# A planned order searched anew around the w_out loads, and the last output tile evicted in three parts

## The chip, the core and the metric

The kernel runs on one core of a Trainium2 chip. The core has a matrix engine (TensorE, PE in the profile, with its weight loads listed apart as PEld), a vector engine (DVE), a scalar engine (ACT), GpSimd (POOL) and SyncE (SP), which here only issues DMAs. Each engine works through its own list of instructions in order, and waits on semaphores where it needs another engine or a transfer. The metric is the device time of one execution in microseconds (us).

## The reference

A retention layer (attention without softmax, with a decay per head) feeds a two-layer feed-forward network. 8 batches, 8 heads, 576 positions, head size 64; 4608 tokens of width 512; the hidden width is 2048.

```python
scores = scale * np.matmul(q, k.transpose(0, 1, 3, 2))
gamma = 1.0 - 2.0 ** (-5.0 - np.arange(H))
rel = pos[:, None] - pos[None, :]
Dmat = np.where(rel >= 0, gamma[:, None, None] ** rel[None], 0.0)
x = np.matmul(scores * Dmat, v)        # then [B, H, S, D] -> [B*S, H*D]
h = x @ w_in                           # 512 -> 2048
g = np.where(h > 0, h, np.exp(np.minimum(h, 0)) - 1)
out = g @ w_out                        # 2048 -> 512, float32
```

## The kernel before

**Attention.** The sequence is cut into stretches of 256 positions (and a rest of 64 for each batch, gathered four batches at a time). Decay is put into q and k as powers of gamma, so that a stretch needs only masked scores, values and a running state. The first two batches are cut once more, into eight "units" u0 to u7 of 256 positions by four heads: u0 and u1 are the two halves of the first stretch, u2 and u3 of the second, u4 to u7 the same for the second batch. A unit n is made by these steps: loads `ldq`, `ldk`, `ldv` (256 KB each, issued by SP into raw tiles `r`); scaled casts `cq0`, `cq1` of q (line 559), plain casts `kk0`, `kk1` of k (568) and scaled casts `vs0`, `vs1` of v (582); a transposition, which for u0 to u4 is done on PE (`Tn_0`, `Tn_1`, line 605, copied out of PSUM as `cp`, line 611) and for u5 to u7 by a transposing DMA (`tr5` to `tr7`, line 594, issued by SP); then scores `sc`, state `st` and output `iv` on PE, a mask on DVE (965), sums of the state and their casts `us` and `ub` (916, 886, 904), and copies of the result into x, `xc` (1001). From u4 on, these PE steps are merged: A4 begins u4, A5 ends u4 and begins u5, iv5 ends u5, A6 begins u6, A7 ends u6 and begins u7.

**Feed-forward.** Tokens are worked on in 16 blocks: 14 of 256 tokens (4 of them made of units), the last two of 512. `F1_b_p` (function `ffn1`) multiplies block b by a slice of w_in into one PSUM bank; ACT takes the exponential, ACT or DVE the other branch, DVE joins them into g. `F2_b_t_c_n` (function `ffn2`) multiplies 128 tokens (tile t) of g by w_out rows from 128c on, 4 chunks of 128 rows at a time, and adds up over 16 such chunks. The sum is copied out of PSUM by ACT or DVE (`oc`, line 1179) and stored by SP (`so`, line 1187). The last tile of the last block is done in two halves of 256 columns. `rows_of` gives the pieces in which a tile is stored: one of 128 rows, or two of 64 for the gathered rests.

**Weights.** w_in comes in five DMAs (`wi0` to `wi4`) and w_out in four (`wo0` to `wo3`, 512 KB each in bf16), all issued by POOL, which makes their descriptors in software. F1 with p = 0 needs `wi0`, p = 1 `wi1`, p = 2 and 3 `wi2`, p = 4 and 5 `wi3`, the rest `wi4`. F2 with c = 0, 4, 8, 12 needs `wo0`, `wo1`, `wo2`, `wo3`.

**What sets the order.** `Plan.run` (line 73 on) is a list scheduler in the program itself. At build time it gives every step a start by assumed costs, and the emitted program is the list of steps of each engine in that order. `AT` gives steps an earliest start in the plan, `RANKS` moves their priority. Both shape only the order of each engine's list: on the chip an engine takes the next instruction as soon as its semaphores allow. Where the plan sees PE idle in the first 50 us, it puts in matmuls on zeros ("fillers", lines 1273 to 1277), with which PE stays busy.

**Holds.** `HOLD = {"ldq4": "wo0", "ldq6": "wo1"}` delays two loads on the chip: POOL copies one column of the named part of `w_out_sb` into the raw tile (line 403), so this copy waits until that part has landed, and the load into the same tile waits for the copy. SP issues in order, so all later loads wait behind a held one. POOL's list in this stretch is: ... `wi4`, `vs0_3`, `wo0`, `wo1`, `wo2`, hold of ldq4, tables for the later stretches (iotas and a mask, lines 515 to 526), hold of ldq6, `wo3`, then the casts of u4.

PE's list up to the end of the units begins: 7 matmuls on zeros ("warm"), T0, T1, sc0, st0, sc1, iv0, st1, iv1, T2, st2, T3_0, sc2, T3_1, F1_0_0, F1_0_1, iv2, sc3, st3, F1_0_2, F1_0_3, iv3, F1_0_4, F1_0_5, then F1 of block 1 and the rest of block 0, F2 of blocks 0 and 1 with T4, A4, A5, iv5 between them, F1_2_0, A6, F1_2_1 and so on.

Of the kernel before, what the change touches and what calls it, by code (L numbers as in the profile page):

```python
# [17 lines left out]
P = 128  # L18
# [17 lines left out]
class Plan:  # L36
# [6 lines left out]
    def add(self, *a, **kw):  # L43
        op = Op(*a, **kw)
        self.ops.append(op)
        for key in op.use:
            self.users.setdefault(key, []).append(op)
            op.turn += self.owner.get(key, [])
        for cls, key, *_ in op.take:
            self.owner[key] = [op]  # L50
            if cls not in FREE:
                op.turn += self.takers.get(cls, [])
                self.takers[cls] = [op]
        return op
# [152 lines left out]
JOINT = True  # L207
BD_ACT = 0.6
FILL = 0.6
TWO, STEP = 2, 4  # L210
KK = {"ACT": 0.37}
VV = {"POOL": 0.62, "DVE": 0.5}
# [15 lines left out]
UAPART = (5, 7)  # L228
HOLD = {"ldq4": "wo0", "ldq6": "wo1"}
VLATE = (0, 1)  # L230
AT = {"wi0": 7.1, "wi1": 8.0, "wi2": 8.5, "wi3": 11.0, "wi4": 15.0, "wo0": 16.4, "wo1": 16.1, "wo2": 19.3, "wo3": 31.3, "so_0_1_0_0": 74, "so_1_0_0_0": 74, "so_1_1_0_0": 74, "so_2_0_0_0": 76, "so_2_1_0_0": 81.47, "F2_3_1_0_0": 78.57, "g_2_6": 63.17, "md_3_3": 66.87, "md_1_7": 35.82, "us5_0": 44.11, "ex_2_4": 55.85, "ex_2_2": 53.77, "xc1_u4": 43.93, "xc0_4": 82.16, "g_1_3": 27.7, "xc1_u3": 22.43, "F2_3_0_8_0": 78.02, "md_0_7": 36.11, "F1_6_6": 119.86, "tr0_5": 66.58, "md_2_2": 56.94, "ex_6_5": 119.61, "md_0_1": 21.97, "mask1_7": 117.16, "md_0_5": 25.96, "F2_4_0_8_0": 93.26, "cv7": 47.1, "F1_0_5": 22.04, "cq11": 5.73, "ub5_1": 47.68, "F1_0_3": 19.14, "g_1_7": 36.97, "vs1_7": 47.23, "cq00": 4.92, "cq16": 39.58, "ex_0_3": 22.04, "kk1_4": 33.96, "tr6": 42.78, "md_1_0": 25.42}
RANKS = {"us1_0": -2, "F1_0_1": 4, "mask0_7": 2, "g_2_1": -2, "md_3_3": 8, "A7": -4, "cv1_5": -4, "cv1_6": 4, "mask1_u6": 8, "so_5_0_0_0": -8, "md_0_2": -8, "ex_2_7": 2, "xc0_u7": -8, "F1_2_6": -8, "A4": 2, "F2_3_0_4_0": -8, "ub0_0": -4, "kk1_2": 4, "g_0_5": 4, "F2_1_1_0_0": 8}
FREE = ("f", "e", "em", "g", "ot")
SURE = 3
ATT = ((0, 0), (0, 1), (1, 0), (1, 1), (2, 0), (2, 1), (3, 0), (3, 1), (4, 0), (4, 1), "X",
# [12 lines left out]
def kernel(  # L248
# [12 lines left out]
    B, H, S, D = q.shape  # L261
    DM, DF = moe_w_in.shape
    HP = H // 2
    C = 64
    NC = 4
    R = C // 2
    TB = NC * C
# [11 lines left out]
    def mm(*a, **kw):  # L279
        return pin(nc.tensor.matmul(*a, **kw))  # L280
# [54 lines left out]
    add = plan.add  # L335
# [4 lines left out]
    def T(cls, key, shape, dt):  # L340
        return (cls, key, shape, dt)
# [8 lines left out]
    for n, key in enumerate(ATT):  # L350
        it = Work()
# [18 lines left out]
    blocks, place = [], 0  # L370
    for i, keys in enumerate(FFN):
        blk = Work()
# [775 lines left out]
    def rows_of(blk, t):  # L1148
        it, half = blk.its[t // 2], t % 2
        if not it.tail:  # L1150
            return [(0, P, it.b * S + it.T * TB + half * P)]
        return [(j * C, C, (it.b + 2 * half + j) * S + 2 * TB) for j in range(2)]

    tilesof2, byp = [], {}

    def ffn2(blk, t, f0, f1, rank, n0=0, n1=DM):
        pkey, okey = ("p", blk.i, t, n0), ("ot", blk.i, t, n0)
        per, width = 512 // blk.w, n1 - n0
        gs = range(f0 // per, (f1 - 1) // per + 1)

        def emit(op):
            pm = tiles[pkey][:, :width]
            for ft in range(f0, f1):
                g = tiles["g", blk.i, ft // per]
                o = (ft % per) * blk.w + t * P
                mm(pm, g[:, o : o + P], w_out_sb[:, ft, n0:n1], start=(ft == 0), stop=(ft == NFT - 1))

        op = add(f"F2_{blk.i}_{t}_{f0}_{n0}", {"PE": 0.216 * (f1 - f0) * width / DM},
                 [blk.g[p] for p in gs] + [w_out_ld[ft] for ft in range(f0, f1)], emit, rank,
                 take=[] if f0 else [T("f", pkey, [P, DM], FP32)],  # L1170
                 use=([pkey] if f0 else []) + [("g", blk.i, p) for p in gs], after=chain.get(2))
        chain[2] = op
        if f0 == 0:
            tilesof2.append([])
            byp[pkey] = tilesof2[-1]
        byp[pkey].append(op)
        if f1 == NFT:
            def emit_o(op):
                pin(copy[op.eng](tiles[okey][:, :width], tiles[pkey][:, :width]))  # L1179

            oc = add(f"oc_{blk.i}_{t}_{n0}", {"ACT": 0.59 if width == DM else 0.36,
                                              "DVE": (0.66 if width == DM else 0.36, 0.3)}, [op], emit_o, rank,
                     take=[T("ot", okey, [P, DM], FP32)], use=[pkey], banks=[(pkey, 0)])
            for lo, n, i0 in rows_of(blk, t):
                def emit_s(op, lo=lo, n=n, i0=i0):
                    eng = nc.scalar if op.eng == "ACT" else nc.sync
                    pin(eng.dma_start(out[i0 : i0 + n, n0:n1], tiles[okey][lo : lo + n, :width]))

                add(f"so_{blk.i}_{t}_{n0}_{lo}", {OUT: 0.5}, [oc], emit_s, -2, use=[okey],
                    dma=(0.67 * n / P * width / DM, 8))  # L1190
# [38 lines left out]
    for blk in blocks:  # L1229
        base, n = (blk.at + len(blk.its)) * 16 + 1, blk.w // P  # L1230
        if blk.i < TWO:
            for o in blocks[:TWO] if blk.i == TWO - 1 else ():
                o.base = (o.at + len(o.its)) * 16 + 1
            for c in range(0, NFT, STEP) if blk.i == TWO - 1 else ():
                for o in blocks[:TWO]:
                    for t in range(n):
                        ffn2(o, t, c, c + STEP, blocks[0].base + c)
            continue
        for t in range(n):
            last = blk is blocks[-1] and t == n - 1  # L1240
            for n0, n1 in [(0, DM // 2), (DM // 2, DM)] if last else [(0, DM)]:
                for c in range(4):
                    ffn2(blk, t, 4 * c, 4 * c + 4, base + 8 * t + 2 * c, n0, n1)

    named = {op.name: op for op in plan.ops}
    for op, name in holds:
        op.deps.append(named[name])
    for name, t in AT.items():
        if name in named:
            named[name].early = t  # L1250
    for name, shift in RANKS.items():
        if name in named:
# [6 lines left out]
    last = 0.0  # L1259
    for op in order:  # L1260
# [4 lines left out]
        if op.eng == "PE":  # L1265
            gap = op.start - last if op.start < 50 and last else 0.0
            if gap > 0:
# [3 lines left out]
                if op.name.startswith("T"):  # L1271
                    for n in range(int(gap * FILL / (0.107 if op.start < 6 else 0.06))):
                        pin(nc.tensor.transpose(spot[:, n % 4], zero[:, :P], ident))
                elif spot is not None:
                    for _ in range(int(gap * FILL / (0.107 if op.start < 6 else 0.06))):
                        mm(spot[:, :P], zero[:, :P], zero[:, :P], start=True, stop=True)
            last = op.end
# [34 lines left out]
```

## Time and profile before

| | |
|---|---|
| time, median of 3 runs | 298.61 us (298.08 to 298.75) |
| the profiled execution, time | 298.65 us |
| its span in the profile | 296.9 us, so 1.75 us lie outside it |
| PE busy | 289.6 us, 98% of the span |
| DVE, ACT, POOL busy | 200.7, 160.1, 119.8 us |
| granted PE clock | 1.00 in every stretch |

Busy time of PE counts the fillers too. The profile's chain of waits follows the work that ended last back to the start; the timeline lists instructions in order of time, with the idle time before each group and what ended it in brackets.

### The profile page before, as it was taken

What the parts mean: (1) busy time and instruction counts of PE and PEld (TensorE: products, weight loads), DVE (VectorE), ACT (ScalarE), POOL (GpSimd) and SP (SyncE); (2) the same over time, 40 slices, a digit from 0 to 9 for tenths busy, and PEclk for the clock granted to TensorE, in tenths of its full rate; (3) what the DMA queues carried; (4) which work ended last, traced back from release to release, by engine and by line L of the source; (5) the groups of instructions that cost most, each with busy time, mean ns of one, the idle gap of its engine ahead of it and who ended that gap; (6) DMA issues with size and microseconds to landing.
All of it is one profiled execution on the core that took longest, in us unless ns stands there. A gap on an engine that the chain in (4) does not pass through costs nothing.

```text
span 296.9 us, 9161 instructions
## 1 busy us (share of the span) xinstructions
PE 289.6 (98%) x3825; PEld 186.8 (63%) x3825; DVE 200.7 (68%) x374; ACT 160.1 (54%) x299; POOL 119.8 (40%) x193
## 2 busy tenths in 40 slices
PE   7999998999999999999999999999999999999995
PEld 4778644776585866776666677767666444444444
DVE  3878831987775878787786867767876567766500
ACT  5568615774283745656565466454565548544311
POOL 5932675763836544565456347370720000000000
PEclk9999999999999999999999999999999999999999
DMA  7999989999999985799999699976461100011221
GB/s 227 283 207 208 285 230 221 263 243 197 291 241 216 270 191 119 187 233 229 239 202 245 127 230 235 244 131 178 112 109 38 38 35 35 0 38 38 50 91 72
DMA packets 128618, 50.67 MB, mean 171 GB/s; under 512 B 92608, under 2 KB 124096, under 8 KB 128576
## 3 DMA queue, kind: packets, MB, share of 16 engines
q1 hardware_dynamic: 123296, 45.63, 67.4%
q0 software_dynamic: 4752, 4.19, 8.8%
q8 instruction: 30, 0.49, 0.7%
q10 hardware_dynamic: 528, 0.26, 0.3%
q14 instruction: 12, 0.10, 0.1%
HBM read 36.70 MB, written 9.44 MB: 155 GB/s over the span
## 4 chain that ended last, share of the span: by engine, by line
PE 82%; DMA 12%; POOL 3%; SPq 1%; issue 1%; ACT 0%; POOLq 0%; ACTq 0%
PE f L280 82%; DMA r<-in_q_dram 4%; DMA w_out_sb<-in_moe_w_out_dram 4%; DMA r<-in_v_dram 2%; DMA T<-st 2%; POOL w_in_sb L486 1%; POOL vn L582 1%; SPq L392 1%; POOL st L559 1%; SPq L594 0%; ACT ot L1179 0%; POOL r L403 0%; POOLq L559 0%; POOL pos_i L515 0%; ACTq L1179 0%
## 5 line engine op out<-in xcount | busy, mean ns | idle before, releaser
L280 PE MATMUL f<-xt,w_in_sb 128*128 128x256 bf16 (+1 forms) x1024 | 140.1, 286 | 0.3 <-DMA w_in_sb<-in_moe_w_in_dram 0.3
L280 PE MATMUL f<-w_out_sb,g 128*128 128x512 bf16 (+1 forms) x592 | 140.2, 373 | 0.0
L1118 ACT ACTIVATE e<-f 128x512 f32<-128x512 f32 x144 | 85.3, 598 | 76.1 <-PE f L280 74.7
L280 PEld LDWEIGHTS <-w_in_sb 128*128 128x128 bf16 x1024 | 99.4, 98 | 37.6 <-DMA w_in_sb<-in_moe_w_in_dram 0.6
L280 PEld LDWEIGHTS <-g 128*128 128x128 bf16 x592 | 56.7, 98 | 51.4
L1132 DVE TENSOR_SCALAR em<-e 128x512 bf16<-128x512 f32 x84 | 45.0, 538 | 39.5 <-ACT e L1118 39.5
L1142 DVE SCALAR_TENSOR_TENSOR g<-f,em 128x512 bf16<-128x512 f32 x84 | 57.4, 688 | 5.5
L1140 DVE SCALAR_TENSOR_TENSOR g<-e,f 128x512 bf16<-128x512 f32 x60 | 40.3, 681 | 10.0 <-ACT f L1128 9.0
L630 POOL CAST kv<-r 128x512 bf16<-128x512 f32 x28 | 17.0, 629 | 48.7 <-issue 26.5
L1179 ACT COPY ot<-f 128x512 f32<-128x512 f32 (+1 forms) x37 | 21.3, 576 | 26.5 <-PE f L280 26.2
L650 POOL TENSOR_TENSOR kv<-r,gq 128x512 bf16<-128x512 f32 x28 | 29.3, 1067 | 12.7 <-DMA r<-in_q_dram 12.7
L650 POOL TENSOR_TENSOR kv<-r,gk 128x512 bf16<-128x512 f32 x28 | 29.5, 1063 | 8.5 <-DMA r<-in_k_dram 8.5
L1128 ACT ACTIVATE f<-f 128x512 f32<-128x512 f32 x54 | 32.2, 598 | 0.0
L1001 ACT CAST xt<-f 128x512 bf16<-128x512 f32 (+1 forms) x36 | 20.7, 624 | 19.5 <-PE f L280 19.4
L969 DVE TENSOR_TENSOR pt<-f,mask 128x512 bf16<-128x512 f32 x28 | 18.0, 679 | 3.0 <-PE f L280 3.0
L954 POOL CAST bd<-S 128x256 bf16<-128x256 f32 x41 | 16.0, 405 | 9.8 <-ACT S L940 5.1
L942 DVE TENSOR_TENSOR S<-f,S 128x256 f32<-128x256 f32 x36 | 15.1, 419 | 3.2 <-PE f L280 1.2
L965 DVE TENSOR_TENSOR pt<-f,mask_u 128x512 bf16<-128x512 f32 x16 | 10.3, 682 | 8.5 <-PE f L280 8.5
L280 PEld LDWEIGHTS <-kv 64*64 64x64 bf16 x832 | 10.8, 104 | 0.1
L280 PE MATMUL f<-T 64*64 64x64 bf16 (+1 forms) x576 | 9.6, 199 | 1.2 <-DMA T<-st 1.2
L559 POOL TENSOR_TENSOR st<-r,gq 128x256 bf16<-128x256 f32 x14 | 8.8, 645 | 4.0 <-DMA r<-in_q_dram 3.9
L280 PEld LDWEIGHTS <-T 64*64 64x64 bf16 x576 | 7.3, 108 | 2.3 <-DMA T<-st 1.4
(67 smaller groups left out, 123.5 us busy)
## 6 DMA issues: line engine op xcount, KB each, us to landing
r<-in_v_dram SPq DMA_DIRECT2D x32, 256.0 KB, 4.5
r<-in_k_dram SPq DMA_DIRECT2D x31, 256.0 KB, 4.3
out_dram<-ot SPq DMA_DIRECT2D x31, 256.0 KB, 2.9
r<-in_q_dram SPq DMA_DIRECT2D x12, 512.0 KB, 4.6
r<-in_q_dram SPq DMA_DIRECT2D x8, 256.0 KB, 4.3
w_out_sb<-in_moe_w_out_dram POOLq DMA_DIRECT2D x4, 512.0 KB, 11.5
w_in_sb<-in_moe_w_in_dram POOLq DMA_DIRECT2D x3, 512.0 KB, 9.1
out_dram<-ot SPq DMA_DIRECT2D x10, 128.0 KB, 2.2
```

Source lines behind the costliest of these rows:

```text
L280: return pin(nc.tensor.matmul(*a, **kw))
L630: pin(copy[op.eng](heads(tiles[nkey][:, VS[s]]), tiles["rv", n][:, s * H : (s + 1) * H]))
L650: pin(alu[op.eng].tensor_tensor(tiles[nkey][:, 2 * i + j].rearrange("p (y x d) -> p x y d", y=2, x=HP), raw.rearrange("p (x y) d -> p x y ...
L954: pin(copy[op.eng](tiles[bkey], tiles[skey]))
L969: pin(nc.vector.tensor_tensor(pt.rearrange("p h s n -> p (h s) n"), src.rearrange("p (h n) -> p h n", n=C), mask.rearrange("p e r -> p (e ...
L1001: pin(copy[op.eng](dst, src))
L1118: pin(nc.scalar.activation(tiles[ekey], tiles[hkey], AF.Exp))
L1128: pin(nc.scalar.activation(ph, ph, AF.Relu))
L1132: pin(alu[op.eng].tensor_scalar_add(em, e, -1.0))
L1140: pin(nc.vector.scalar_tensor_tensor(g, e, -1.0, ph, ALU.add, ALU.min))
L1142: pin(nc.vector.scalar_tensor_tensor(g, ph, 0.0, tiles[mkey], ALU.max, ALU.min))
L1179: pin(copy[op.eng](tiles[okey][:, :width], tiles[pkey][:, :width]))
```

## The change

Constants (only the entries that differ are shown, one to a line):

```diff
+HALVED, LAST = 3, [(0, 256), (256, 384), (384, 512)]
 AT = {
-  "wi2": 8.5, "wo0": 16.4, "wo1": 16.1, "wo2": 19.3, "wo3": 31.3, "F1_0_3": 19.14,
+  "wi2": 8.8, "wo0": 16.7, "wo1": 15.8, "wo2": 19.9, "wo3": 31.1,
+  "ub4_1": 43.87, "T0_0": 8.14, "md_0_0": 19.36, "xc0_u0": 13.99, "T4_0": 35.06,
+  "cp1_1": 10.22, "md_0_3": 23.9, "kk0_0": 5.92, "cp4_1": 38.78,
...
 RANKS = {
+  "xc1_u1": 4, "md_0_3": -2, "md_1_4": -2, "F1_1_0": 8, "cp4_0": 2, "tr7": -8, "cq17": 2, "g_1_6": 8,
...
```

Code:

```diff
     def rows_of(blk, t):
         it, half = blk.its[t // 2], t % 2
         if not it.tail:
-            return [(0, P, it.b * S + it.T * TB + half * P)]
+            i0 = it.b * S + it.T * TB + half * P
+            if (blk.i, t) in halved:
+                return [(j * C, C, i0 + j * C) for j in range(2)]
+            return [(0, P, i0)]
         return [(j * C, C, (it.b + 2 * half + j) * S + 2 * TB) for j in range(2)]
+
+    halved = [(b.i, t) for b in blocks for t in range(b.w // P)][-1 - HALVED : -1]
...
-            oc = add(f"oc_{blk.i}_{t}_{n0}", {"ACT": 0.59 if width == DM else 0.36,
+            oc = add(f"oc_{blk.i}_{t}_{n0}", {"ACT": 0.14 + 0.45 * width / DM,
...
-            for n0, n1 in [(0, DM // 2), (DM // 2, DM)] if last else [(0, DM)]:
+            for n0, n1 in LAST if last else [(0, DM)]:
```

In the emitted lists this makes the following differences; from A6 on to the last tiles the lists of all engines are the same as before.

- PE: the first tiles are transposed in the order T1_0, T0_1, T1_1, T0_0; the states st0 and st1 stand ahead of the scores sc0 and sc1; T2 and T3_0 ahead of iv0. Then F1_0_0, iv2, sc3, st3, F1_0_1, F1_0_2, iv3, F1_0_3, F1_0_4 and so on. T4_0 and T4_1 stand together behind four F2 with c = 0, and A4 behind all four F2 with c = 4. There are 10 fillers more (44 for 34): 21 before T1_0, where 7 stood before T0_0; none is left behind F1_0_0. The last tile takes 48 matmuls for 32.
- POOL: `ub0_1` and `ub1_1` stand where `vs1_1` and cq of u2 stood; the weights are issued in the order `wo1`, `vs1_3`, `wo0`, `wo2`; the tables come ahead of both holds, and then the hold of ldq4 (for `wo0`), the hold of ldq6 (for `wo1`) and `wo3` follow one another. `ub4_0` stands behind the four casts of u6 instead of after the second, `ub4_1` behind cq of u7.
- ACT and DVE share the copies of T, the casts of k and the state sums of u0 to u3 in another way; DVE copies T4_1 out, which ACT did.
- SP: the loads keep their order. At the end, 14 stores of 64 rows, one of 128 rows by 256 columns and two of 128 by 128, for 8 of 64 rows, three of 128 by 512 and two of 128 by 256.

More of the change, by code (lines that the diff above doesn't have):

```diff
@@ L230 @@
 VLATE = (0, 1)
-AT = {"wi0": 7.1, "wi1": 8.0, "wi2": 8.5, "wi3": 11.0, "wi4": 15.0, "wo0": 16.4, "wo1": 16.1, "wo2": 19.3, "wo3": 31.3, "so_0_1_0_0": 74, "so_1_0_0_0": 74, "so_1_1_0_0": 74, "so_2_0_0_0": 76, "so_2_1_0_0": 81.47, "F2_3_1_0_0": 78.57, "g_2_6": 63.17, "md_3_3": 66.87, "md_1_7": 35.82, "us5_0": 44.11, "ex_2_4": 55.85, "ex_2_2": 53.77, "xc1_u4": 43.93, "xc0_4": 82.16, "g_1_3": 27.7, "xc1_u3": 22.43, "F2_3_0_8_0": 78.02, "md_0_7": 36.11, "F1_6_6": 119.86, "tr0_5": 66.58, "md_2_2": 56.94, "ex_6_5": 119.61, "md_0_1": 21.97, "mask1_7": 117.16, "md_0_5": 25.96, "F2_4_0_8_0": 93.26, "cv7": 47.1, "F1_0_5": 22.04, "cq11": 5.73, "ub5_1": 47.68, "F1_0_3": 19.14, "g_1_7": 36.97, "vs1_7": 47.23, "cq00": 4.92, "cq16": 39.58, "ex_0_3": 22.04, "kk1_4": 33.96, "tr6": 42.78, "md_1_0": 25.42}
@@ L232 @@
-RANKS = {"us1_0": -2, "F1_0_1": 4, "mask0_7": 2, "g_2_1": -2, "md_3_3": 8, "A7": -4, "cv1_5": -4, "cv1_6": 4, "mask1_u6": 8, "so_5_0_0_0": -8, "md_0_2": -8, "ex_2_7": 2, "xc0_u7": -8, "F1_2_6": -8, "A4": 2, "F2_3_0_4_0": -8, "ub0_0": -4, "kk1_2": 4, "g_0_5": 4, "F2_1_1_0_0": 8}
+AT = {"wi0": 7.1, "wi1": 8.0, "wi2": 8.8, "wi3": 11.0, "wi4": 15.0, "wo0": 16.7, "wo1": 15.8, "wo2": 19.9, "wo3": 31.1, "so_0_1_0_0": 74, "so_1_0_0_0": 74, "so_1_1_0_0": 74, "so_2_0_0_0": 76, "so_2_1_0_0": 81.47, "F2_3_1_0_0": 78.57, "g_2_6": 63.17, "md_3_3": 66.87, "md_1_7": 35.82, "us5_0": 44.11, "ex_2_4": 55.85, "ex_2_2": 53.77, "xc1_u4": 43.93, "xc0_4": 82.16, "g_1_3": 27.7, "xc1_u3": 22.43, "F2_3_0_8_0": 78.02, "md_0_7": 36.11, "F1_6_6": 119.86, "tr0_5": 66.58, "md_2_2": 56.94, "ex_6_5": 119.61, "md_0_1": 21.97, "mask1_7": 117.16, "md_0_5": 25.96, "F2_4_0_8_0": 93.26, "cv7": 47.1, "F1_0_5": 22.04, "cq11": 5.73, "ub5_1": 47.68, "g_1_7": 36.97, "vs1_7": 47.23, "cq00": 4.92, "cq16": 39.58, "ex_0_3": 22.04, "kk1_4": 33.96, "tr6": 42.78, "md_1_0": 25.42, "ub4_1": 43.87, "T0_0": 8.14, "md_0_0": 19.36, "xc0_u0": 13.99, "T4_0": 35.06, "cp1_1": 10.22, "md_0_3": 23.9, "kk0_0": 5.92, "cp4_1": 38.78}
@@ L233 @@
+RANKS = {"us1_0": -2, "F1_0_1": 4, "mask0_7": 2, "g_2_1": -2, "md_3_3": 8, "A7": -4, "cv1_5": -4, "cv1_6": 4, "mask1_u6": 8, "so_5_0_0_0": -8, "md_0_2": -8, "ex_2_7": 2, "xc0_u7": -8, "F1_2_6": -8, "A4": 2, "F2_3_0_4_0": -8, "ub0_0": -4, "kk1_2": 4, "g_0_5": 4, "F2_1_1_0_0": 8, "xc1_u1": 4, "md_0_3": -2, "md_1_4": -2, "F1_1_0": 8, "cp4_0": 2, "tr7": -8, "cq17": 2, "g_1_6": 8}
 FREE = ("f", "e", "em", "g", "ot")
```

## The prediction

> **What bounds the kernel now.** I read the page first: busy shares, then the chain that ended last.
>
> ```profile
> span 296.9 us, 9161 instructions
> PE 289.6 (98%) x3825; PEld 186.8 (63%) x3825; DVE 200.7 (68%) x374; ACT 160.1 (54%) x299; POOL 119.8 (40%) x193
> PE 82%; DMA 12%; POOL 3%; SPq 1%; issue 1%; ACT 0%; POOLq 0%; ACTq 0%
> ```
>
> PE is full, and 82% of the chain is PE; but 15% is DMA and POOL, so there is a stretch in which transfers set the pace. The chain in order of time shows where it ends:
>
> ```profile
> 7.04 0.86 POOL vn L582
> ...
> 25.93 0.19 POOL r L403
> ...
> 26.15 5.93 DMA r<-in_q_dram
> ...
> 44.40 6.29 DMA T<-st
> ...
> 50.73 8.02 PE f L280 x152
> ...
> 58.79 171.01 PE f L280 x2692
> ...
> 229.84 63.76 PE f L280 x356
> ...
> 293.67 0.37 ACT ot L1179
> ```
>
> Up to 50.69 us the chain is the hold of ldq4 (line 403), the loads of u4 to u6, and the transposition `tr6`, for which A6 waits. From 50.73 to 293.60 it is PE without a break. So the time is the start of A6, plus 242.9 us of matmuls, plus the tail. PE's timeline before A6:
>
> ```profile
> 14.87 1.91 PE L280 MATMUL f<-xt,w_in_sb 128*128 128x256 bf16 x16
> 16.71 0.25 PE L280 MATMUL f<-T,s 64*64 64x128 bf16 x4
> ...
> 18.19 1.92 PE L280 MATMUL f<-xt,w_in_sb 128*128 128x256 bf16 x16
> 20.04 0.25 PE L280 MATMUL f<-T,s 64*64 64x128 bf16 x4
> ...
> 21.15 1.05 PE L280 MATMUL f<-xt,w_in_sb 128*128 128x256 bf16 x8 [0.28 <-DMA w_in_sb<-in_moe_w_in_dram]
> ...
> 42.43 0.32 PE L280 MATMUL f<-vn,st 64*64 64x64 bf16 x16
> ...
> 48.53 1.04 PE L280 MATMUL f<-xt,w_in_sb 128*128 128x256 bf16 x8
> 50.73 0.42 PE L280 MATMUL f<-T 64*64 64x128 bf16 x16 [1.16 <-DMA T<-st]
> ...
> 51.20 2.79 PE L280 MATMUL f<-xt,w_in_sb 128*128 128x256 bf16 x24
> ```
>
> PE is through F1_2_0 at 49.57 and idles 1.16 us until `tr6` is there. Two conclusions: a head in which PE is up to 1.16 us later costs nothing, and a better one brings nothing unless `tr6` lands earlier. A second gate stands at 21.15, where F1_0_4 waits for `wi3`.
>
> **The change part by part.** *Units u0 to u3.* The work is the same in another order, so what counts is whether PE still reaches F1_0_4 by 21.15. The longest new chain is ACT's list:
>
> ```profile
> 4.62 0.71 ACT L568 CAST st<-r 128x256 bf16<-128x256 f32 x2 [1.48 <-DMA r<-in_k_dram]
> 6.79 0.58 ACT L611 COPY T<-f 128x512 bf16<-128x512 bf16 x1
> ...
> 8.56 0.27 ACT L886 COPY mid<-f 128x128 f32<-128x128 f32 x1
> ...
> 9.91 0.81 ACT L1001 CAST xt<-f 128x256 bf16<-128x256 f32 x2 [0.76 <-PE f L280]
> ```
>
> st0 still waits for `vs1_0`, at 7.04 to 7.9 us as `vs0_0` before, so ACT's `ub0_0` starts near 8.5. Then come one state copy, 6 `cp`, 4 `kk` and 3 `xc` before F1_0_0: 0.27 + 6 x 0.54 + 4 x 0.36 + 3 x 0.40 = 6.15, at 14.65, where F1_0_0 began at 14.87 before. (A 0.58 that follows another costs some 0.04 less, since it overlaps.) To F1_0_4 it is four F1 (two take 1.91 - 0.13 = 1.78) and iv2, sc3, st3 (16.71 to 18.19) and iv3 (from 20.04, done by 20.87, since PE then idles 0.28 up to 21.15): 14.65 + 3.56 + 1.48 + 0.83 = 20.5, before 21.15. The 10 fillers more are 10 x 0.057 = 0.6 us by the rows of 128 columns below; they lie ahead of waits that remain, and without that cover 20.5 + 0.6 is still 21.1. The weights' own issue slips by some 0.1 us (`wi3` behind `ub0_1`, `ub1_1`, two casts), while the queue ahead of it is full. I take 0.
>
> *Tables ahead of the holds, T4 behind four F2, `ub4_0` behind u6's casts.* The tables move from behind the first hold into the 8.28 us in which POOL idles ahead of it (row of 25.93 below), and lose the 2 us or so between the two holds. F2 and T4 change places and cost the same. A5, which begins at 42.43, needs `ub4_0`:
>
> ```profile
> 41.32 0.29 POOL L904 CAST s<-mid 128x128 bf16<-128x128 f32 x1
> ```
>
> Moved behind a cast of q and one of k (0.37, half of the 0.74 below, and some 0.6), it ends near 42.5: at most 0.2 us of PE, covered by the 1.16 at A6. If that cover is gone it costs its 0.2.
>
> *`wo0` behind `wo1`.* This is the edit that touches the chain. The hold of ldq4 now waits for the second w_out DMA. POOL's rows give both landings:
>
> ```profile
> 25.93 0.19 POOL L403 CAST r<-w_out_sb 128x1 f32<-128x1 bf16 x1 [8.28 <-DMA w_out_sb<-in_moe_w_out_dram]
> ...
> 28.84 0.19 POOL L403 CAST r<-w_out_sb 128x1 f32<-128x1 bf16 x1 [0.81 <-DMA w_out_sb<-in_moe_w_out_dram]
> 29.30 0.79 POOL L497 DMA_DIRECT2D w_out_sb<-in_moe_w_out_dram  x1 [0.26 <-issue]
> ...
> 38.13 0.74 POOL L568 CAST st<-r 128x256 bf16<-128x256 f32 x2 [1.72 <-DMA r<-in_k_dram]
> ```
>
> So ldq4, and with it all nine loads of u4 to u6 on SP, is issued 2.9 us later, at 29.05 for 26.15. Whether that reaches `tr6` hangs on what the loads did in those 2.9 us. The DMA queues between 26.2 and 28.9 us, then 29.1 to 32.6, then 30.2 to 32.6 (packets, MB, share):
>
> ```profile
> q0 software_dynamic: 552, 0.55, 124.1%
> ...
> ```
>
> ```profile
> q1 hardware_dynamic: 1879, 0.94, 90.1%
> ```
>
> ```profile
> q1 hardware_dynamic: 1549, 0.77, 107.6%
> ```
>
> Nothing: until 28.9 us SP's queue (q1) moved not one packet, for POOL's queue (q0) filled the engines with w_out, which POOL had issued long before. Issued at 29.05, the loads can start moving about 30.2 (in the tail below, 0.8 us pass from issue to first packet; I allow 1.15). They lose what moved from 29.1 to 30.2, 0.94 - 0.77 = 0.17 MB, 0.5 us at the 335 GB/s of the last window. That is the upper end. The lower is 0: a transfer has landed when the slowest of the 16 engines has done its share. `wo2` was issued at 16.9, as this row of its issue has it (size, us to landing):
>
> ```profile
> w_out_sb<-in_moe_w_out_dram POOLq DMA_DIRECT2D x1, 512.0 KB, 14.8
> ```
>
> So it landed at 31.6, and ldq4 at 26.15 + 5.93 = 32.08: on the slowest engine the loads waited for w_out until 31.6 anyway, and can be there 1.4 us earlier in the changed kernel too. `wo3` is issued at 29.3 to 29.5 as before, the engines stay busy, and the bytes that must pass up to ldk5, which frees POOL's cast at 38.13, are the same. Being nearest to this row, I take 0.0 for `tr6`; behind ldk5 two casts, `tr5`, five loads and `tr6` follow in the same order.
>
> By the Trainium skill (DMA: Bandwidth & Descriptors, "Queues, rings and completion order") an engine takes turns between its queues packet by packet, which would have given ldq4 about half the engines from 27.3 on and made the 2.9 us count, at the price of the second rival below; the trace disagrees, with no packet of q1 before 28.9 us.
>
> *The tail.* One part of 256 columns becomes two of 128. Pace and parts (matmuls of 256 columns above; the transpositions have 128 columns and a weight load each; eviction, then two stores by their size and time to landing):
>
> ```profile
> 12.75 0.62 PE L605 MATMUL f<-ident,st 128*128 128x128 bf16 x8
> ...
> 33.54 0.39 PE L605 MATMUL f<-ident,st 128*128 128x128 bf16 x4
> ```
>
> ```profile
> out_dram<-ot SPq DMA_DIRECT2D x1, 256.0 KB, 2.0
> ```
>
> ```profile
> out_dram<-ot SPq DMA_DIRECT2D x1, 128.0 KB, 1.7
> ```
>
> 256 columns: (2.79 - 1.04) / 16 = 0.109 each, 16 take 1.75. 128 columns: (0.62 - 0.39) / 4 = 0.057, 32 take 1.84, +0.09; the last one drains 0.05 faster: +0.04. Last eviction 0.37 (chain) to 0.27 (row of line 886): -0.10. Last store 64 KB: from 256 to 128 KB the time to landing fell by 0.3, half of that again is -0.15 (bounds 0 and -0.3). Sum -0.2, between -0.06 and -0.36. The part before it has the 0.9 us of the last part's matmuls for its own eviction (0.27) and issue. In the window from 294.04 to the end, in slices of 0.074 us, the store issued at 294.06 moves in the 12th to 18th:
>
> ```profile
> DMA  0000000000027999620000000000000000000000
> ```
>
> The engines are empty before, so the tiles stored in halves, whose second issue ends over 2 us earlier, take nothing from it, and SP has nothing else to issue: 0.
>
> **The sum.** Profiled execution 298.65 + 0.0 + 0.0 - 0.2 = 298.45; it lies 0.04 above the median, so 298.4.
>
> **The rivals.** *Faster: A6 no longer waits.* If `tr6` lands early, up to 1.16 us go, and 297.3 is reached. For it: with no load in its way `wo2` ends sooner, and `wo3` may meet fewer loads; the name of the edit says that the last quarter of w_out goes behind the loads of u6, and if its 2.9 us (25.93 to 28.84, one such transfer) came behind ldk5, `tr6` would be that much earlier and PE the bound. Against it: in POOL's list `wo3` stands right behind the hold of ldq6 in both kernels and waits for no load, so the edit doesn't do what it is called; and `tr5` still waits for ldk5.
>
> *Slower: the hold's 2.9 us reach A6.* The place is SP's list: behind ldq4 stand eight loads, then `tr5`, five loads and `tr6`. Were all of them 2.9 us later, 298.45 + 2.9 = 301.3; beyond 0.8 us of delay it is slower than before by my bound. For it: the chain runs through exactly this hold. Against it: the 0.17 MB above.
>
> *Slower: weight loads set the pace of the narrow parts.* Each 128 columns need a weight load, and the mean load takes 0.098 us:
>
> ```profile
> L280 PEld LDWEIGHTS <-g 128*128 128x128 bf16 x592 | 56.7, 98 | 51.4
> ```
>
> If they didn't overlap, 32 x 0.098 - 1.75 = +1.4 and 299.8. Against it: the transpositions load weights too and keep 0.057. The Trainium skill (TensorE: Matmul & The Clock Gate, "Back-to-back issue gap") gives 81 ns for each matmul of 128 columns in a stream with weight loads, 32 x 0.081 = 2.59, an estimate that would make the sum 299.2; the rows of line 605 disagree.
>
> **How the numbers follow.** About 0.2%, 0.6 us, can be told from no change. Forecast 0.57: 298.4, its own range 297.9 to 298.9. A6 free of its wait 0.25 (297.3 to 297.9). The hold reaches A6 0.13 (299.2 to 301.3), weight loads 0.05. Of the forecast's share 0.03 lie below 298.0. So faster 0.28, same 0.54, slower 0.18. The range: 297.2, the whole wait gone, to 299.7, a hold that passes on 1.2 us.
>
> **What would show it.** Right: A6 starts at 50.7 (to 51.2), preceded by an idle time of PE on `T<-st`; ldq4 is issued near 29.05 and ldk5's cast still runs near 38.1; F1_0_4 starts at 21.15 behind w_in; the end of the span is 3.1 to 3.2 us behind PE's last matmul, for 3.3. Wrong: A6 with no wait before 50 us, or one behind 51.5; 128-column matmuls of the last tile at over 0.06 us each; a new wait of PE between 21 and 49 us.

## The result, and the profile after

The changed kernel takes 302.91 us (median of 6 runs, 301.18 to 303.83) against 298.35 for the one before, run beside it (6 runs, 297.64 to 299.05). The ratio is 1.0144, with an interval of 1.0108 to 1.0180. It is slower, where 298.4 and "same" were predicted. The profiled execution took 302.68 us, 4.03 more than that of before. Its granted PE clock is 0.994 over the whole execution, and that of the five others 0.988 to 0.994, so the fall of the clock that the profile shows below is not peculiar to it.

The page of the changed kernel: busy time of PE, the row of the granted clock in 40 slices, and the chain's shares.

```profile
PE 291.7 (97%) x3851; PEld 187.9 (62%) x3851; DVE 198.5 (66%) x375; ACT 159.8 (53%) x298; POOL 119.7 (40%) x194
...
PEclk9999979999999999999999999999999999999999
...
PE 87%; DMA 8%; POOL 3%; issue 1%; SPq 1%; ACT 0%; POOLq 0%; ACTq 0%
```

One slice of the clock, the sixth (37.6 to 45.1 us), shows a 7 that wasn't there. The chain of waits has changed its course in the same place:

```profile
28.86 0.20 POOL r L404
...
29.36 6.06 DMA r<-in_k_dram
...
35.87 2.71 issue
...
38.62 0.56 POOL vn L583
...
39.63 0.39 PE f L606 x2
40.03 23.08 PE f L281 x312
```

Before, the transfers let go of the chain at A6 (50.73), behind `tr6`. Now they let go at 39.63, at T4_1, the second transposition of k of u4, and from there PE sets the pace to the end. PE's timeline has the stall, what follows it, and A6 (at 55.09, with no idle time in front):

```profile
32.12 3.62 PE L281 MATMUL f<-w_out_sb,g 128*128 128x512 bf16 x16
35.57 0.65 PE L606 MATMUL f<-ident,st 128*128 128x128 bf16 x6
39.63 0.39 PE L606 MATMUL f<-ident,st 128*128 128x128 bf16 x2 [3.42 <-POOL st L569]
39.82 5.11 PE L281 MATMUL f<-w_out_sb,g 128*128 128x512 bf16 x16
...
55.09 0.42 PE L281 MATMUL f<-T 64*64 64x128 bf16 x16
```

Two things cost time here. PE idles for 3.42 us, and the 16 matmuls behind the idle time take 5.11 us where the same 16 took 3.62 at 32.12. The windows say why (from left: busy time and instructions of PE, PEld, DVE, ACT, POOL, then the granted clock, the DMA share and GB/s):

```profile
36.00:39.60 3.60, 0.21 (x2) 0.04 (x2) 2.21 (x4) 0.00 (x0) 0.98 (x3) 0.97 1.07 302
39.60:42.80 3.20, 3.17 (x9) 1.25 (x10) 0.42 (x1) 0.00 (x0) 3.20 (x7) 0.50 0.66 196
42.80:45.00 2.20, 2.20 (x21) 0.94 (x22) 0.00 (x0) 0.00 (x0) 2.17 (x5) 1.00 0.60 136
```

After the idle time the clock is at 0.50, and it is back at 1.00 in the window from 42.8 on. The last few matmuls of the stretch already run at full clock. The loss is 5.11 - 3.62 = 1.5 us.

What T4_1 waited for is in POOL's list (line 560 casts q, 569 k, 583 v):

```profile
28.74 0.31 POOL L404 CAST r<-w_out_sb 128x1 f32<-128x1 bf16 x2 [8.73 <-DMA w_out_sb<-in_moe_w_out_dram]
29.29 0.79 POOL L498 DMA_DIRECT2D w_out_sb<-in_moe_w_out_dram  x1 [0.24 <-issue]
32.09 1.18 POOL L560 TENSOR_TENSOR st<-r,gq 128x256 bf16<-128x256 f32 x2 [2.01 <-DMA r<-in_q_dram]
35.47 0.40 POOL L569 CAST st<-r 128x256 bf16<-128x256 f32 x1 [2.20 <-DMA r<-in_k_dram]
38.62 0.62 POOL L583 TENSOR_TENSOR vn<-r,gk 128x256 bf16<-128x256 f32 x1 [2.74 <-DMA r<-in_v_dram]
39.18 0.40 POOL L569 CAST st<-r 128x256 bf16<-128x256 f32 x1
```

T4_1 needs `kk1_4`, the cast at 39.18. Its data had been there since 35.4. But `vs0_4` stands ahead of it in POOL's list and waits 2.74 us for `ldv4`, which landed at 38.55; before, it had landed at 33.63, and `vs0_4` ran without a wait:

```profile
33.73 0.61 POOL L582 TENSOR_TENSOR vn<-r,gk 128x256 bf16<-128x256 f32 x1
```

`ldv4` is late because of the queues. POOL's queue (q0) carries w_out, SP's queue (q1) the loads. The changed kernel's queues between 29.1 and 32.6 us, the window in which the prediction had counted 0.94 MB of loads before (the first row is the share of the DMA engines in 40 slices of the window, then packets, MB, share):

```profile
DMA  9996644433444386579999999999799989998664
...
q1 hardware_dynamic: 989, 0.50, 49.9%
q0 software_dynamic: 180, 0.17, 33.5%
```

Then from 32.6 to 36 us, first before, then after:

```profile
q0 software_dynamic: 478, 0.48, 83.4%
q1 hardware_dynamic: 640, 0.32, 36.2%
```

```profile
q0 software_dynamic: 442, 0.44, 84.7%
q1 hardware_dynamic: 463, 0.23, 27.3%
```

By 32.6 us SP's queue had moved 0.50 MB for 0.94. The engines were half idle from 29.5 to 30.6 (the 3s to 6s of the first row): most of them were through with w_out and had no load yet. The packets of `wo3`, issued at 29.29 as before, come in from about 31.9 on, and from 32.6 to 36 they take 84.7% of the engines. The 0.44 MB that had moved at some 270 GB/s before (0.94 MB in 3.5 us) now had to pass at some 70 (0.23 MB in 3.4 us). Of u4's loads, q landed at 31.92, no later than before (32.08), k at 35.42 (32.83), and v 3 us behind k.

The span grew by 300.96 - 296.94 = 4.02 us. A6 is 4.36 later, PE takes 0.19 longer from A6 to its end (243.05 for 242.86), and the tail is 0.53 shorter (2.82 us from PE's last matmul to the end of the span, for 3.35).

### The profile page after: what moved, and what is told of

It is laid out like the page before. It is cut to its first block, busy times and chain, and to the rows that moved or that the text cites. A ratio compares the mean times of both kernels' runs of the same rounds, so it can differ in the third digit from the quotient of the medians.

```text
span 301.0 us, 9215 instructions
## 1 busy us (share of the span) xinstructions
PE 291.7 (97%) x3851; PEld 187.9 (62%) x3851; DVE 198.5 (66%) x375; ACT 159.8 (53%) x298; POOL 119.7 (40%) x194
## 4 chain that ended last, share of the span: by engine, by line
PE 87%; DMA 8%; POOL 3%; issue 1%; SPq 1%; ACT 0%; POOLq 0%; ACTq 0%
PE f L281 86%; DMA w_out_sb<-in_moe_w_out_dram 4%; DMA r<-in_k_dram 2%; DMA r<-in_v_dram 2%; POOL vn L583 1%; SPq L393 1%; POOL w_in_sb L487 0%; POOL st L560 0%; POOL st L569 0%; POOL w_out_sb L498 0%; PE f L606 0%; POOL s L905 0%; ACT ot L1185 0%; PE f L1279 0%; POOL r L404 0%
## 5 line engine op out<-in xcount | busy, mean ns | idle before, releaser
L281 PE MATMUL f<-w_out_sb,g 128*128 128x512 bf16 (+2 forms) x608 | 141.5, 371 | 0.0
L281 PEld LDWEIGHTS <-w_in_sb 128*128 128x128 bf16 x1024 | 99.3, 98 | 37.6 <-issue 0.3
L281 PEld LDWEIGHTS <-g 128*128 128x128 bf16 x608 | 57.4, 98 | 52.7 <-issue 1.9
L1133 DVE TENSOR_SCALAR em<-e 128x512 bf16<-128x512 f32 x84 | 42.3, 504 | 39.8 <-ACT e L1119 39.6
L1185 ACT COPY ot<-f 128x512 f32<-128x512 f32 (+2 forms) x38 | 21.4, 564 | 26.4 <-PE f L281 25.3
L631 POOL CAST kv<-r 128x512 bf16<-128x512 f32 x28 | 16.5, 611 | 44.8 <-issue 26.1
L651 POOL TENSOR_TENSOR kv<-r,gk 128x512 bf16<-128x512 f32 x28 | 29.5, 1062 | 8.1 <-DMA r<-in_k_dram 8.1
L583 POOL TENSOR_TENSOR vn<-r,gk 128x256 bf16<-128x256 f32 x12 | 7.6, 644 | 4.1 <-DMA r<-in_v_dram 4.1
L560 POOL TENSOR_TENSOR st<-r,gq 128x256 bf16<-128x256 f32 x12 | 7.6, 650 | 3.7 <-DMA r<-in_q_dram 3.7
```

Source lines behind the costliest of these rows:

```text
L631: pin(copy[op.eng](heads(tiles[nkey][:, VS[s]]), tiles["rv", n][:, s * H : (s + 1) * H]))
L651: pin(alu[op.eng].tensor_tensor(tiles[nkey][:, 2 * i + j].rearrange("p (y x d) -> p x y d", y=2, x=HP), raw.rearrange("p (x y) d -> p x y ...
L1133: pin(alu[op.eng].tensor_scalar_add(em, e, -1.0))
```

## The experiments

Three theories were told apart first. **S**: the whole loss comes from `wo0` behind `wo1`, because the loads, released 2.8 us later, meet `wo3`. **H**: the rest of the new head (the order of u0 to u3, T4 together, `ub4_0` later) costs the time. **R**: the late release alone costs it, whatever else is on the queues. Later runs asked for the share of each step, and **Q**, **D** and **N** concern the tail. Steps were moved in the finished order with these lines, and the pairs below are what stood in the list:

```diff
     order = plan.run(...)
+    for name, behind in [("wo1", "wo0")]:
+        order.remove(named[name])
+        order.insert(order.index(named[behind]) + 1, named[name])
```

**1. The changed kernel with `wo1` behind `wo0` again** (the pair above).

> The changed kernel with one exchange: wo0 is again issued ahead of wo1, all else as changed. Theory S (squeeze): the loads of u4 to u6 must move between the release of ldq4's hold and wo3's data (about 32.6 us); released at 28.7 us only q and k of u4 get through, ldv4 lands behind wo3, and POOL's list holds vs0_4, kk1_4 and so T4_1 of PE behind it. With wo0 first the hold ends near 25.9 again: ldv4 lands near 33.6, T4_1 waits under 0.2 us, A6 waits for tr6 near 50.7 as before, and the tail keeps its 0.5 us: 297.8 to 298.2 us. Rival H (the new order of u0 to u3, of T4 and of ub4_0 costs the time): it stays at 301 to 303 us.

297.28 us (10 runs) against 297.83 of the kernel before (19 runs), ratio 0.9959 (0.9928 to 0.9990). POOL's and PE's rows:

```profile
26.17 0.19 POOL L404 CAST r<-w_out_sb 128x1 f32<-128x1 bf16 x1 [6.07 <-DMA w_out_sb<-in_moe_w_out_dram]
...
34.43 0.61 POOL L583 TENSOR_TENSOR vn<-r,gk 128x256 bf16<-128x256 f32 x1
```

```profile
35.51 0.61 PE L606 MATMUL f<-ident,st 128*128 128x128 bf16 x8
35.96 3.62 PE L281 MATMUL f<-w_out_sb,g 128*128 128x512 bf16 x16
...
49.82 0.42 PE L281 MATMUL f<-T 64*64 64x128 bf16 x16
```

The loads are released at 26.4, `vs0_4` finds its data, all eight transpositions run in one go, and A6 starts at 49.82 without a wait. H falls: everything else in the change is kept, and the kernel is the fastest so far. All ten executions have a granted clock of 0.999 or 1. Set against the changed kernel, A6 is 55.09 - 49.82 = 5.27 us earlier: the F2 behind T4 start 39.82 - 35.96 = 3.86 earlier and take 1.49 less, and -0.08 remains. A6's own wait for `tr6` was expected to come back and did not; experiment 7 comes to that.

**2. The kernel before with `wo0` behind `wo1` and the hold of ldq4 behind the tables** (pairs `wo0` behind `wo1`, `holdldq4` behind `iota`), so that the hold, the second hold and `wo3` follow one another as in the changed kernel.

> The kernel before with two moves in POOL's list: wo1 is issued ahead of wo0, and ldq4's hold stands behind the tables, so that both holds and wo3 follow one another as in the changed kernel. Theory S: the whole loss comes without any of the other edits: ldv4 lands near 38.5 us, PE waits about 3 us at T4_1, its granted clock falls to a half for about 3.4 us, 302.3 to 303.3 us (the tail is the old one). Rival H: 298.2 to 298.8 us.

302.72 us (4 runs), ratio 1.0158 (1.0116 to 1.0199). The stall, behind the same cast:

```profile
40.62 0.28 PE L605 MATMUL f<-ident,st 128*128 128x128 bf16 x2 [4.46 <-POOL st L568]
40.74 4.44 PE L280 MATMUL f<-w_out_sb,g 128*128 128x512 bf16 x12
```

These two moves alone make the whole loss. `ldv4` landed at 39.52, and the 12 matmuls behind the stall took 4.44 us, with the clock at 0.5 for 3.4 of them.

**3. The kernel before with `wo0` behind `wo1` alone.** The tables stay between the two holds, which puts off the issue of `wo3` by 2 us, to 31.25.

> The kernel before with wo1 issued ahead of wo0 and nothing else: ldq4 is released as late as in the changed kernel (28.8 us), but the tables (2 us of POOL) stay between the two holds, so wo3 is issued about 2 us later, near 31.2, and its data come near 34.4. Theory S: the loads get some 2 us more before wo3, ldv4 lands by 34.6 and T4_1 waits under 1 us; 298.2 to 299.4 us. Rival R (the late release alone costs it, whatever wo3 does): 2.9 us and the clock's fall, 301 to 303 us.

299.93 us (4 runs), ratio 1.0063 (1.0040 to 1.0087). The hold ran at 28.78, as late as in experiment 2. R falls: with `wo3` 2 us later, `ldv4` landed at 34.50, and there was no stall at T4 and no fall of the clock. The time, 0.5 us more than S allowed, is lost in two other places:

```profile
31.22 1.92 PE L280 MATMUL f<-xt,w_in_sb 128*128 128x256 bf16 x16 [0.68 <-DVE g L1140]
...
44.86 0.42 PE L280 MATMUL f<-T 64*64 64x128 bf16 x16 [0.90 <-DMA T<-st]
```

```profile
30.11 0.20 DVE L532 CAST pos<-pos_i 128x7 f32<-128x7 int32 x1 [2.14 <-POOL pos_i L521]
```

The first is no transfer: the tables stand behind the late hold in POOL's list, DVE waits 2.14 us for them, and its part of g comes behind that wait. PE's 0.68 us are the larger part of what F2 is late by (32.98, for 31.81 before). The second is A5's wait for `tr5`, which stands in the chain of waits:

```profile
37.97 6.85 DMA T<-st
```

`tr5`, issued at 37.97, takes 6.85 us to land, for 3.3 in experiment 1 (39.48 to 42.74), since the loads ahead of it now meet `wo3` (landed at 40.07). The collision was moved on, not removed.

**4. The changed kernel with `wo3` behind `cq14`**, the second cast of q of u4, so that it is issued at 33.45.

> The changed kernel with wo3 moved behind the casts of q of u4 (cq14) in POOL's list, about 4 us later; the hold still ends near 28.7. Theory S: no packet of wo3 before 36 us, ldv4 lands at 33.5 to 34.6, T4_1 waits under 0.7 us, ldk5 lands ahead of wo3, so tr6 is there by 49.5 and A6's wait goes: 297.0 to 298.0 us, faster than the kernel before. Rival R: 301 to 303 us. Rival W (wo3 now is late itself): F2 with c = 12 waits for it behind 43 us, over 298.5 us.

299.21 us (10 runs), ratio 1.0056 (1.0031 to 1.0081): a miss in size. `ldv4` landed at 34.60 and T4 ran without a stall, so `wo3` is the transfer that held it back. That is the profiled execution; three of the ten have a granted clock of 0.989 to 0.994 (300.0 to 301.9 us), and where these lost time is not in the record. But now `ldk6` was behind `wo3` (both landed at about 43), as PE's row of A5 and POOL's rows show:

```profile
44.86 0.24 PE L281 MATMUL f<-T,s 64*64 64x128 bf16 x2 [2.01 <-POOL s L905]
```

```profile
43.25 0.40 POOL L569 CAST st<-r 128x256 bf16<-128x256 f32 x1 [1.91 <-DMA r<-in_k_dram]
...
44.51 0.30 POOL L905 CAST s<-mid 128x128 bf16<-128x128 f32 x1
```

`ub4_0` (line 905), which the change put behind the casts of u6, is now late by their wait, and A5 waits 2.01 us for it. That move was costed at up to 0.2 us; it is worth that only while `ldk6` is on time.

**5. The changed kernel with `vs0_4` behind `kk1_4`**, which takes the cast for T4_1 out from behind the wait for v.

> The changed kernel with vs0_4 moved behind kk1_4 in POOL's list, so that the second cast of k of u4, which T4_1 needs, no longer stands behind a cast that waits for ldv4. The transfers stay as they are (ldv4 near 38.5 us). Theory S, its POOL part (an instruction queued behind a waiting one): T4_1 starts near 36.3 instead of 39.6 us, PE's clock does not fall, A4 then waits for the casts of v until about 40; A5 next waits for tr5 (near 44.4), A6 starts near 51.6 instead of 55.1: 299.0 to 300.2 us. If PE was held by the transfers alone, 302 to 303.5.

300.29 us (10 runs) against 298.30 (19 runs), ratio 1.0073 (1.0043 to 1.0104).

```profile
38.16 0.63 PE L606 MATMUL f<-ident,st 128*128 128x128 bf16 x4 [2.72 <-POOL st L569]
```

```profile
37.70 0.74 POOL L569 CAST st<-r 128x256 bf16<-128x256 f32 x2 [4.62 <-DMA r<-in_k_dram]
```

The stall is 2.72 us for 3.42, and the clock did not fall behind it; in two of the ten executions (302.27 and 302.35 us) the granted clock is 0.994, as in the changed kernel. T4_1 was expected at 36.3; here `ldk4` itself came late (37.65, for 35.42 in the profile of the changed kernel), so k too can end up behind `wo3`. The order in POOL's list accounts for part of the stall only. How large a part stays open, since k and v landed close together in this execution (37.65 and 38.21), and in the profile of the changed kernel 3 us apart.

**6. The changed kernel with PE kept busy before T4_1.** 58 transpositions of zeros are added, whose results nothing uses.

```diff
             last = op.end
+        if op.name == "T4_1":
+            for n in range(58):
+                pin(nc.tensor.transpose(tiles[fresh[0]][:, n % 4], zero[:, :P], ident))
         op.emit(op)
```

> The changed kernel with 58 transpositions of zeros put in ahead of T4_1 on PE (about 3.2 us of work where PE idles). The wait of T4_1 stays to 39.6 us, but PE is busy in it. Theory C (the half clock from 39.4 to 42.8 us is a second cost, which follows from the idle time): no fall of the clock, the 16 matmuls behind T4_1 take 3.6 instead of 5.1 us, 301.0 to 301.6 us. Rival (the clock's fall has another cause or hides behind a transfer): 302.5 to 303.3.

300.82 us (4 runs), ratio 1.0096 (1.0063 to 1.0130).

```profile
35.78 3.40 PE L1286 MATMUL f<-ident,zero 128*128 128x128 bf16 x58
...
40.31 0.28 PE L606 MATMUL f<-ident,st 128*128 128x128 bf16 x2 [1.01 <-POOL st L569]
40.43 3.62 PE L281 MATMUL f<-w_out_sb,g 128*128 128x512 bf16 x16
```

The transposition that had to wait starts no earlier (40.31), but the 16 matmuls take 3.62 us again. The clock is a cost of its own: 1.5 us in the rows, and 1.4 by the two ratios to the kernel before (1.0144 and 1.0096), which come from different sets of runs. The granted clock is 0.999 or 1 in all four executions.

**7. The tail alone in the kernel before** (the three code edits of the change, the old `AT` and `RANKS`).

> The kernel before with the tail's edits alone (three parts, three tiles in halves, the planner's cost of the eviction). From PE's last matmul to the end of the span 2.8 instead of 3.3 us, made up of 0.10 (eviction), 0.18 (landing of the last store) and 0.2 (fewer semaphores left to check behind the last landing): 297.2 to 297.7 us if A6 waits as before. Rival (only the prediction's terms): 0.2 to 0.3.

297.54 us (10 runs), ratio 0.9963 (0.9927 to 0.9999). PE's end to the end of the span is 2.84 us, as in the changed kernel (2.82). This ratio and that of experiment 1 (0.9959) agree, so the rest of the new head is worth little either way; the intervals leave some 0.3% open. A6 starts at 49.59 here, with no wait. A repeat, which was to store a fourth tile in halves, turned out to be the same program, since that tile is a gathered rest and was in halves already:

> The same with four tiles in halves instead of three: one more store, so the last store uses the first of SP's eight DMA semaphores instead of the eighth, and at the end SP checks the other seven behind its landing. Theory (order of the final checks): 2.8 + 7 x 0.06 = 3.2 us from PE's last matmul to the end. Rival (the halves help by draining earlier): 2.8 us or less.

297.17 us in one run, 2.84 us of tail, A6 at 49.55 with no wait. The wait of A6 for `tr6` is thus a matter of the execution: with the same lists up to the tail, it is there in three of five profiles (1.16 us in that of before, 0.90 and 1.12 in experiment 8) and not in the two here.

**8. What in the tail brings the time.** In the trace SP ends the program with checks of its eight DMA semaphores, one after another in a fixed order, some 0.06 us each. The last store's semaphore is the fourth of them in the kernel before, and the eighth and last after the change. First the kernel before with the last tile in three parts and no tile in halves (`HALVED = 0`), then with three tiles in halves and the last tile in two parts as before.

> The kernel before with the last tile in parts of 256, 128 and 128 columns, and no other tile stored in halves. Theory Q: of the 0.53 us that the tail gained, about 0.28 come from the smaller last part (eviction 0.37 to 0.27, last store's issue to landing 1.68 to 1.52) and 0.25 from the place of the last store's semaphore in SP's closing checks, which the number of stores before it decides. This kernel has one store more than the one before, so its last store comes to the semaphore behind 106: from PE's end to the end of the span 3.0 us (2.95 to 3.06), for 3.35 before and 2.84 with the halves. Rival D, the tiles stored in halves help because they drain earlier: 3.05 to 3.1 us. Rival N, the halves do nothing at all: 2.80 to 2.88 us. Time 296.8 to 298.2 us, which alone tells none of them apart.

> The kernel before with three of the last tiles stored in halves of 64 rows, and the last tile in two parts of 256 columns as before. Theory Q: eviction 0.37 and landing 1.68 as before, the last store on a semaphore further on in SP's closing checks, so landing to end falls by 0.15 to 0.25 us and PE's end to the end of the span is 3.1 to 3.2 us. Theory N, the halves do nothing: 3.33 to 3.38 us. Rival D, earlier drain: issue to landing of the last store below 1.6 us. Time 296.9 to 298.4 us.

| from PE's last matmul to the end | before | three parts only | halves only | both |
|---|---|---|---|---|
| place of the last store's semaphore | 4th | 5th | 7th | 8th |
| last eviction, us | 0.37 | 0.27 | 0.37 | 0.27 |
| total, us | 3.35 | 3.02 | 3.16 | 2.84 |

Q gave 3.0 and 3.1 to 3.2; D and N both fall. With the halves alone the last store still lands 1.68 us after its issue, so it isn't that the engines drain earlier; from its landing to the end it is 1.007 us for 1.187, three places of 0.06.

In the time of the first of the two, 300.58 us in its one run, there is more than was expected (up to 298.2). Its tail is as forecast; its head was disturbed: `wo0` released `ldq4` at 28.14 us instead of near 26.2, with no edit to the head, A5 waited 0.94 us and A6 1.12, and A6 started at 52.90. The halves-only kernel took 298.74 in its one run (expected up to 298.4), with a wait of 0.90 us at A6. The kernel before took 297.67 in one run beside them.

## Why the prediction was wrong

**The step that failed is "`wo0` behind `wo1`", costed at 0.0 with an upper end of 0.5 us.** Its first half held: ldq4 was issued at 28.95 (predicted 29.05), and nothing of the loads had moved before 28.9 in either kernel. So did the argument from the slowest engine, for the load that it was made for: ldq4 landed at 31.92 for 32.08. What failed is the sentence "`wo3` is issued at 29.3 to 29.5 as before, the engines stay busy, and the bytes that must pass up to ldk5 [...] are the same".

- *The engines did not stay busy.* Against 0.17 MB allowed, 0.44 MB less had moved by 32.6 us (0.50 for 0.94). Up to 30.2 the loss was the one allowed (0.01 MB for 0.17). But from 30.2 to 31 the loads were still coming up to speed (0.14 for 0.24), and from 31.6 to 32.6 `wo3` was already coming in (0.16 for 0.33). The slowest engine had w_out until 31.1, when `wo2` landed, but most of the others had none from 29.5 on; in the kernel before, these moved loads in that time. The argument from the slowest engine looked at one landing and not at the bytes.
- *The bytes were priced at the wrong rate.* 335 GB/s is what moved from 30.2 to 32.6 us before, when the loads had the engines nearly to themselves. After 32.6 us `wo3` was there, and SP's queue got some 70 GB/s. At that rate 0.44 MB would be 6 us; `ldv4`, at 38.55 for 33.63, is 4.9 late. The row of q0 and q1 between 26.2 and 28.9, quoted in the prediction (0.55 MB to none), had shown this very thing, and it was used for the transfers ahead of the loads and not for the one behind them.
- *The wrong consumer was watched.* The step followed the loads to `tr6` and ldk5, 12 us on, where the old chain ran. The first one hurt was `ldv4`, and through POOL's list, where `vs0_4` stands ahead of `kk1_4`, it stopped T4_1. "A new wait of PE between 21 and 49 us" was named as a sign of being wrong, and 3.42 us came there.
- *A delay was taken to cost its own length*, in the slower rival too (298.45 + 2.9). The clock added 1.5 us. That it falls with a long idle time was not in any bound.

Experiment 2 shows that this step, with the hold behind the tables, is the whole loss; experiment 3 that without that second move, and so without `wo3` at its heels, the late release costs two fifths of it (ratios 1.0063 and 1.0158), part of that through the tables. Experiment 4 shows that `wo3` is what holds `ldv4` back, 6 what the clock does; what POOL's list does was followed in the rows, and 5 leaves its share open. The rival "the hold's 2.9 us reach A6" (up to 301.3, chance 0.13) had the right edit and the right sign, but not the mechanism: it had all loads shift by the same 2.9 us. The first load did not shift at all, `ldk4` by 2.6, `ldv4` by 4.9, and ldk5 by 1.7, since by then `wo3` was through (it landed at 38.36).

**A6's wait.** "A head in which PE is up to 1.16 us later costs nothing" was read from one execution. The cover was there in that one (A6 went from 50.73 with the wait to 55.09 without), but experiments 1 and 7 show A6 at 49.6 to 49.8 with no wait. The rival "A6 no longer waits" is thus true of some executions of the kernel before as well (two of five profiles).

**Units u0 to u3: 0.** Nearly right, but not by its working. F1_0_0 began at 15.69 where 14.65 was worked out, and PE reached F2 0.3 us later than before (32.12 for 31.81); in experiment 1 A6 is 0.23 later than in experiment 7 with the old head (49.82, 49.59). PE's waits of the whole span, largest first, no longer list one for w_in.

```profile
PE f L606 <- POOL st L569: 3.4, 1, 3.4
PE f L281 <- DVE zero L286: 1.3, 1, 1.3
PE f L606 <- ACT st L569: 0.9, 1, 0.9
```

**Tables, T4, `ub4_0`: up to 0.2, hidden.** Right in the changed kernel with the old order of w_out (experiment 1), with two conditions that weren't stated. `ub4_0` costs 2.0 us when `ldk6` is late (experiment 4). And with the late release, the tables ahead of the hold are what lets `wo3` be issued right behind the first loads (experiments 2 and 3): the parts were costed one by one, and the loss needs two of them.

**The tail: -0.2, between -0.06 and -0.36.** The sign was right, the size too small: -0.53 from PE's last matmul to the end. Eviction and store came out as costed, 0.37 to 0.27 and 1.69 to 1.52, and so did PE's +0.04 (in experiment 1 its last stretch of the chain takes 63.80 us for 63.76). The term that was missing is SP's closing checks: from the last landing to the end of the span 0.935 us for 1.187, -0.25. Halved tiles were costed at 0 because they take no bandwidth; they count because they move the last store to another semaphore. The rival of the weight loads falls; the last tile's 32 matmuls of 128 columns, by form:

```profile
L281 PE MATMUL f<-w_out_sb,g 128*128 128x128 bf16 x32 | 1.9, 219 | 0.0
```

That is 0.06 us each with a weight load for each.

## What to carry to other kernels

When a load is held back, price the bytes that it loses at the rate that it will get beside whatever is queued next, not at the rate that it had before, and look at the first consumer and at what stands behind it in an in-order list. A big transfer issued by POOL belongs where the loads of the next step are already through: moving its issue by 2 to 4 us (experiments 3 and 4) only chose which load was hit. A wait seen in a single profile is no cover until a second execution shows it too. And a long idle time of PE has to be priced with the half clock that can follow it.

## What the runs showed of the hardware

**POOL's queue holds SP's back.** Between 33 and 35 us of the changed kernel both queues had work; SP's own rows show that, as it took 4.38 us over one issue:

```profile
33.25 4.38 SPq L393 DMA_DIRECT2D r<-in_q_dram  x1
```

```profile
q0 software_dynamic: 303, 0.31, 101.6%
q1 hardware_dynamic: 98, 0.05, 12.1%
```

Three packets of POOL's queue, of about 1 KB, went for each of SP's, of 0.5 KB: six times the bytes. The Trainium skill (DMA: Bandwidth & Descriptors, "Queues, rings and completion order") has an engine take turns between its queues packet by packet; this window as a whole does not show turns. Later stretches do; experiment 3 from 36.8 to 38 us:

```profile
q0 software_dynamic: 164, 0.17, 83.7%
q1 hardware_dynamic: 164, 0.08, 34.2%
```

There it is packet for packet, with half the bytes for SP. In the changed kernel it is 218 to 38 from 33 to 34.4 us and 114 to 86 from 34.4 to 35.2. Why the turns set in late stays open: whether SP's packets were ready at each engine at each moment is not in the trace.

**The clock goes by fixed steps.** In the traces' record of the granted clock, every change lies on a grid of 3.413 us: in the changed kernel the stretches at one clock last 34.13, 3.41 and 259.41 us, which is 10, 1 and 76 steps. In these traces it follows PE's busy share of one such step. The steps around the stalls, with a share of 0.06 (35.99 to 39.41 us of the changed kernel) and 0.22 (37.95 to 41.36 of experiment 2), were followed by a step at half clock. So were steps of 0.10 to 0.35 at the last matmul of four other profiles (experiments 4, 6, 7 and 8). Once the clock was full, steps of 0.45 and more never were, in the twelve profiles; one of them is that of 33.89 to 37.30 us in experiment 5, in which most of its idle 2.72 us lie. So no length of idle time decides by itself: it matters where on the grid it falls. The limit lies between 0.35 and 0.45 here, as far as the modelled ends of the matmuls allow. The Trainium skill (TensorE: Matmul & The Clock Gate, "Part 1: The HAM clock gate") puts both the idle time that throttles and the time to warm up at one window of about 3.4 us; the length agrees, but in these runs the window need not be idle throughout.

**The head varies between executions.** With the same order of the head, `ldq4` was released between 26.1 and 28.1 us (experiments 7 and 8), and A6 started between 49.55 and 52.90. What made `wo0` land 2 us later in one of these executions (27.88 us, for 25.84 to 26.20 in the four others) was not tried.

The fastest kernels here are those of experiments 1 and 7, 0.4% below the kernel before; the tail is what they share. By the rows it is worth 0.5 us, or 0.16%; the rest may be A6's wait, which neither profile has, and lies within the intervals.
